# Attention with a coarse path, then a gated mixture of experts: v by one transfer for each head, coarse rows spread by one-hot products, constants from small bands

## The chip, the cores and the metric

One core of a Trainium2 chip runs the whole program. The metric is the device time of one execution in microseconds (us), lower is better. Fast runs of one kernel in one set of rounds agree within about 1.5%; between sets, on the same or another chip, the median of the kernel before moved. So kernels are compared by their ratio to the kernel before, run in the same rounds on the same chip.

The engines, as the page of the changed kernel shows them: PE runs 7566 products (PEld is its loading of weights, as many), DVE 470, ACT 403 and POOL 319 other instructions (sums, copies, casts, exponentials), SP only issues transfers here (DMA). Each engine works off its own list of instructions in order; in the changed kernel, for example, ACT stands still for 20.7 us before one copy of a constant, with later work behind it.

## The reference, cut to what matters

```python
# q, k, v: 8 batches x 8 heads x 576 rows x 64
q_d, k_d, v_d = means of four neighbouring rows            # 144 coarse rows
out_up    = repeat(softmax_attention(q_d, k_d, v_d), 4)    # each coarse row serves four queries
out_local = softmax_attention(q, k, v, mask=|i - j| < 4)
x = (out_up + out_local) as 4608 rows of 512
e = argmax(x @ w_gate)                                     # one of 8 experts for each row
out[row] = softmax weight * sigmoid(x @ w_output_gate)[e] * (relu(x @ w1[e]) @ w2[e])
```

A wrong argmax sends a row to another expert. The kernel therefore carries most operands as a high and a low half of 16 bits.

## The kernel before

A unit is two heads of one batch: 32 units, four for each batch. Queries are cut into ten windows, and each window needs at most 64 rows of k and v. A list scheduler in the Python code fixes the order of all tasks on all engines when the program is built. The parts that matter:

```python
def load_v(u):                       # 6 transfers for a unit, issued by SP
    for h in range(2):
        for w0, w1, n in ((0, 9, 2), (1, 2, 4), (5, 6, 4)):
            nc.sync.dma_start(vf[r, w0:...:w1 - w0, :], ...)

def upsample(b, t):                  # 10 transfers for a batch, also issued by SP:
    for w in (2 * t, 2 * t + 1):     # each normalised coarse row is copied to four queries
        nc.sync.dma_start(t_up[r:r + 4 * (j1 - j0), t, :], _ap(src, [src.ap[0], [0, 4], [1, Dm]]))

def x_sum(b, t):                     # mostly on POOL
    (nc.vector if t in XS_DVE else nc.gpsimd).tensor_tensor(x, x, t_up[:, t], op=ALU.add)

def make_mask():                     # 20 selects of POOL, then 22 more and 11 memsets for the means
    for w in range(NW):
        nc.gpsimd.affine_select(out=reg, ...); nc.gpsimd.affine_select(out=reg, ...)
# ... cut: casts and turns of q and k, means of v, scores, exponentials, values, gating, experts
```

The softmax here doesn't subtract the row's maximum and nothing guards it: scores larger than these inputs give would overflow.

## Time and profile before

| | kernel before |
|---|---|
| median of its runs | 543.5 us (539.1 to 546.8) |
| profiled execution | span 562.9 us, marked slow |
| first to last exponential | 32.66 to 338.86 us, 9.88 us a unit |
| last exponential to first product of the experts | 56.4 us |
| experts | 167.7 us |

There is one exponential pair for each unit, so the time between two of them is the pace of the attention. The profile's chain of work that ended last goes back from the last instruction and says at each step what released it. Its shares by engine (SPq is time in which a transfer was being issued, "issue" is time in which an engine waited for nothing that the profile shows):

```profile
PE 31%; DMA 17%; issue 17%; DVE 12%; POOL 10%; SPq 8%; ACT 2%; another core or an unknown queue 1%; POOLq 0%; DVEq 0%; ACTq 0%
```

A quarter of the whole span is transfers and their issue.

### The profile page before, as it was taken

To read this page: it belongs to the slowest core of one execution; us is meant where nothing else is said; L and a number is where in the kernel's file an instruction comes from. 1 tells how busy PE (TensorE), PEld (TensorE's weight loads), DVE (VectorE), ACT (ScalarE), POOL (GpSimd) and SP (SyncE) were. 2 spreads that over 40 slices of the span, in tenths; PEclk is the share of its full clock that TensorE was granted. 3 is DMA by queue.
4 is the path that set the end of the run, shared out by engine and by line. 5 is a ranking of instruction groups with operands and counts; after the bars stand their busy time and mean duration, and the time that the engine had idled before them with its cause. 6 is when DMAs were issued, how large, how long until landed. Compare 5 with 4: busy or idle time off the path is not lost.

```text
span 562.9 us, 17377 instructions
## 1 busy us (share of the span) xinstructions
PE 399.3 (71%) x7470; PEld 291.4 (52%) x7470; DVE 261.9 (47%) x480; ACT 227.4 (40%) x397; POOL 274.0 (49%) x351
## 2 busy tenths in 40 slices
PE   0457858548846869764778974530899999999992
PEld 0356746446634667653567753430655665565560
DVE  1457537329467665639655774431322332232220
ACT  0255444444624545633446562330233333333331
POOL 8863236319365655546746357484053345323312
PEclk9999795787865876975887786555799999999997
DMA  8569878988866984797853041513189999992202
GB/s 172 131 128 251 214 190 207 185 192 160 186 129 146 185 169 116 154 171 153 206 112 91 13 79 70 86 43 113 42 177 193 209 188 223 193 223 98 110 29 74
DMA packets 92743, 81.74 MB, mean 145 GB/s; under 512 B 49693, under 2 KB 80413, under 8 KB 92656
## 3 DMA queue, kind: packets, MB, share of 16 engines
q1 hardware_dynamic: 74736, 49.55, 38.6%
q0 software_dynamic: 17920, 30.98, 26.8%
q8 instruction: 60, 0.98, 0.7%
q14 instruction: 27, 0.22, 0.1%
HBM read 68.23 MB, written 21.05 MB: 159 GB/s over the span
## 4 chain that ended last, share of the span: by engine, by line
PE 31%; DMA 17%; issue 17%; DVE 12%; POOL 10%; SPq 8%; ACT 2%; another core or an unknown queue 1%; POOLq 0%; DVEq 0%; ACTq 0%
DMA vf<-in_v_dram 8%; PE pu L689 8%; PE py L699 6%; SPq L398 5%; DMA t_up<-xo 5%; POOL out_dram L702 3%; SPq L236 3%; PE ps L310 3%; PE t L261 2%; PE po L359 2%; PE pd L287 2%; PE ps L312 2%; DMA qk<-in_q_dram 2%; DVE xo L387 2%; POOL hx_xs L517 2%
## 5 line engine op out<-in xcount | busy, mean ns | idle before, releaser
L242 POOL CAST qk<-qk 96x768 f16<-96x768 f32 x64 | 59.1, 945 | 52.0 <-PE t L264 40.3
L402 POOL TENSOR_TENSOR xo<-xo,t_up 128x512 f32<-128x512 f32 x32 | 41.1, 1292 | 74.3 <-DMA t_up<-xo 74.1
L689 PE MATMUL pu<-xgT,w1sb 128*128 128x320 f16 x512 | 72.4, 303 | 1.7 <-DVE xgT L681 0.9
L699 PE MATMUL py<-w2sb,hs 128*128 128x512 f16 x320 | 70.4, 379 | 0.0
L702 POOL DMA_INDIRECT out_dram<-y,xg x40 | 39.7, 993 | 59.1 <-ACT y L701 57.3
L261 PE MATMUL t<-pm,qk 96*128 96x144 f16 x384 | 44.7, 268 | 27.6 <-POOL qk L242 19.4
L689 PEld LDWEIGHTS <-w1sb 128*128 128x128 f16 x512 | 50.7, 99 | 22.6 <-issue 2.7
L408 POOL TENSOR_TENSOR t_xl<-xo,xh 128x512 f16<-128x512 f32 x40 | 47.4, 1200 | 26.9 <-ACT xh L405 26.7
L692 ACT ACTIVATE hs<-pu 128x320 f16<-128x320 f32 x64 | 28.0, 438 | 68.3 <-PE pu L689 60.8
L328 ACT ACTIVATE eh<-ps 128x1008 f16<-128x1008 f32 x32 | 32.3, 1011 | 48.6 <-PE ps L310 41.5
L694 DVE TENSOR_SCALAR hs<-pu 128x320 f16<-128x320 f32 x64 | 31.5, 492 | 43.0 <-PE pu L689 36.6
L699 PEld LDWEIGHTS <-hs 128*128 128x128 f16 x320 | 31.3, 98 | 36.5
L681 DVE COPY xgT<-tp 128x1024 f16<-128x1024 f16 (+1 forms) x24 | 13.0, 595 | 74.7 <-PE py L699 60.1
L261 PEld LDWEIGHTS <-qk 96*128 96x128 f16 x384 | 31.4, 116 | 30.6 <-POOL qk L242 19.4
L701 ACT ACTIVATE y<-py,xg 128x512 f32<-128x512 f32 x40 | 27.5, 688 | 47.9 <-PE py L699 47.9
L517 POOL DMA_INDIRECT hx_xs<-xh,pos x40 | 40.0, 1001 | 12.1 <-issue 9.9
L287 PEld LDWEIGHTS <-pv 64*128 64x128 f16 x1280 | 27.8, 108 | 33.7 <-issue 31.2
L287 PE MATMUL pd<-t_vh,pv 64*128 64x64 f16 x640 | 31.1, 211 | 18.7 <-DVE vdl L299 8.1
L334 DVE TENSOR_TENSOR el<-ps,eh 128x1008 f16<-128x1008 f32 x32 | 38.4, 1200 | 7.9 <-ACT ps L329 6.6
L287 PE MATMUL pd<-vl,pv 64*128 64x64 f16 x640 | 30.9, 211 | 11.0 <-issue 7.4
L387 DVE TENSOR_TENSOR xo<-po,rs 128x448 f32<-128x448 f32 x64 | 36.9, 618 | 1.5
L203 POOL DMA_DIRECT2D w1sb<-in_moe_w_dram x16 | 11.9, 750 | 49.7 <-PE pu L689 49.7
(118 smaller groups left out, 870.3 us busy)
## 6 DMA issues: line engine op xcount, KB each, us to landing
qk<-in_q_dram SPq DMA_DIRECT2D x32, 288.0 KB
qk<-in_k_dram SPq DMA_DIRECT2D x32, 288.0 KB
vf<-in_v_dram SPq DMA_DIRECT2D x128, 64.0 KB
w1sb<-in_moe_w_dram POOLq DMA_DIRECT2D x16, 512.0 KB
w2sb<-in_moe_w_dram POOLq DMA_DIRECT2D x16, 512.0 KB
t_up<-xo SPq DMA_DIRECT2D x48, 120.0 KB
hx_xs<-zt SPq DMA_DIRECT2D x8, 645.0 KB
xg<-hx_xs SPq DMA_DIRECT2D x8, 645.0 KB
```

What stands on the lines that cost most here:

```text
L242: nc.gpsimd.tensor_copy(t16.rearrange("p m h d -> p h m d"), d["f", i])
L261: nc.tensor.matmul(tf[:, S // 2:S // 2 + SD], lhsT=t16[:, m, :], rhs=pm[:, m, :], start=(m == 0), stop=(m == 5), skip_group_check=True)
L287: nc.tensor.matmul(pd[:, h, c:c + D], lhsT=pv[r, w, :], rhs=m[r, w, 0:D], start=(w == 0 and i == 0), stop=(w >= NW - 2 and i == 1), skip_g ...
L328: nc.scalar.activation(d["eh"], ps, AF.Exp, scale=scale)
L334: nc.vector.tensor_tensor(d["el"], d["ps"][:, :, 0:NH], d["eh"], op=ALU.subtract)
L387: nc.vector.tensor_tensor(xo_s[b][:, :, c:c + D], po[:, h, :, 0:D], _bc(rs[:, h], D), op=ALU.mult)
L402: (nc.vector if t in XS_DVE else nc.gpsimd).tensor_tensor(x, x, t_up[:, t], op=ALU.add)
L408: nc.gpsimd.tensor_tensor(t_xl[:, t], xo_s[b][:, t, :], xh_s[b % 4][:, t, 0:Dm], op=ALU.subtract)
L517: ins = nc.gpsimd.indirect_dma_start(out=xs_dram.ap(), out_offset=bass.IndirectOffsetOnAxis(ap=gs[n]["pos"][:, c:c + 1], axis=0), in_=xh_s ...
L689: nc.tensor.matmul(pu[:, 0:c1 - c0], lhsT=w1sb[:, c, 128 * f:128 * f + 128], rhs=xgT[:, c, c0:c1], start=(c == 0), stop=(c == 3))
L699: nc.tensor.matmul(py, lhsT=hs[:, f, 128 * j:128 * j + 128], rhs=w2sb[:, f, :], start=(f == 0), stop=(f == NG - 1))
L702: ins = nc.gpsimd.indirect_dma_start(out=out_rows, out_offset=bass.IndirectOffsetOnAxis(ap=xgi[:, j, Dm // 2 + 1:Dm // 2 + 2], axis=0), in ...
```

## The change

The intent: fewer and simpler things on SP's queue, so that a load never stands behind the spreading of a finished batch. Ten windows of 57 queries (60 at the ends) put the rows of v at equal steps, so one transfer serves a head. The coarse rows reach their queries by products with one-hot matrices. The mask and the means come from one small band each. With it came a re-tuned order, shared tiles in PE's result memory (PSUM), both copies of the turned q and k on ACT, and part of the last batch's work moved from POOL to DVE.

```diff
-QN = [60, 56, 58, 58, 56, 56, 58, 58, 56, 60]
+QN = [60] + [57] * 8 + [60]
@@ load_v
-            for w0, w1, n in ((0, 9, 2), (1, 2, 4), (5, 6, 4)):
-                nc.sync.dma_start(vf[r, w0:w0 + (w1 - w0) * (n - 1) + 1:w1 - w0, :], ...)
+                nc.sync.dma_start(vf[r], _ap(s, [[D, 64], [57 * D, NW], [1, D]], -D))
@@ upsample
-            nc.sync.dma_start(t_up[r:r + 4 * (j1 - j0), t, :], _ap(src, [src.ap[0], [0, 4], [1, Dm]]))
+        ms = [(g, x) for g in range(2) if (t, g) in up_m for x in ("xdh", "xdl")]
+        for i, (g, x) in enumerate(ms):
+            nc.tensor.matmul(ps, lhsT=up_m[t, g], rhs=st[x, b][:, g, :], start=(i == 0), ...)
@@ x_sum
-        (nc.vector if t in XS_DVE else nc.gpsimd).tensor_tensor(x, x, t_up[:, t], op=ALU.add)
+        nc.vector.tensor_tensor(x, st.pop(("us", b, t)), x, op=ALU.add)
@@ constants: make_band, make_mask, make_means, spread_means in place of 42 selects with their memsets
+    def make_up():     # six one-hot matrices, five instructions each, on POOL
@@ order and tiles
-    XT_ACT = (1, 3, 4)
+    XT_ACT = (1, 3)
-    ROOM = {"T": 2, "S": 2, "O": 1, ...
+    ROOM = {"T": 2, "S": 3, "xd": 2, ...
... (cut: turn and turned in one tile, the scheduler's priorities, low halves of the last batch)
```

## The prediction

> **What bounds the kernel now.** I read first the page's busy shares and its 40 slices, then the stretches, the chain of work that ended last, and last the waits and the timeline of single engines.
>
> ```profile
> PE 399.3 (71%) x7470; PEld 291.4 (52%) x7470; DVE 261.9 (47%) x480; ACT 227.4 (40%) x397; POOL 274.0 (49%) x351
> PEclk9999795787865876975887786555799999999997
> DMA  8569878988866984797853041513189999992202
> ```
>
> No engine is full. The 40 slices (14.1 us each) show two stages: up to about 390 us attention and gating (32 units of two heads, eight batches of four units), then the experts, where PEclk is 9. The stretches view puts numbers on it (PE, PEld, DVE, ACT, POOL busy, clock, DMA share, GB/s):
>
> ```profile
> 30.00:340.00 310.00, 224.00 (x6133) 181.37 (x6133) 191.62 (x318) 156.17 (x266) 162.16 (x159) 0.78 0.73 155
> 395.00:563.00 168.00, 0.96 0.65 145
> ```
>
> In attention all four engines are busy 50 to 72% of the time, at a clock of 0.78. The change touches only this stage; the 168 us of experts stay. In the chain cut to 33 to 340 us, transfers and their issue lead:
>
> ```profile
> by line: DMA vf<-in_v_dram 15.6%; SPq L398 8.7%; DMA t_up<-xo 8.3%; issue 6.9%; SPq L236 4.7%; PE ps L310 4.7%; PE t L261 4.4%; PE pd L287 3.6%; PE ps L312 3.3%; DMA qk<-in_q_dram 3.2%; PE po L359 3.2%; DVE d L454 2.8%; PE t L264 2.7%; DVE
> ```
>
> vf, t_up, qk and the issues L398 and L236 make 40.5% of 307 us, 124 us. The queue that issues them (SP), its waits, and who waits for it:
>
> ```profile
> L236 SPq DMA_DIRECT2D vf<-in_v_dram x192: 595/614/1698, 3.9 to 304.2; - x192
> L398 SPq DMA_DIRECT2D t_up<-xo x80: 815/848/1505, 75.2 to 362.5; - x80
> SPq L398 <- DVE xo L387: 40.7, 3, 24.0
> POOL xo L402 <- DMA t_up<-xo: 74.1, 19, 11.4
> DVE xo L402 <- DMA t_up<-xo: 48.6, 8, 10.6
> ```
>
> An issue takes 0.61 or 0.85 us whatever its size, so at the medians SP needs 192 x 0.614 + 80 x 0.848 + 64 q/k x 0.43 + 8 fills x 0.69 = 219 us. It is in order: once a batch ten t_up issues wait for the normalised rows and hold back every load behind them. The exponentials show the result (start us, us):
>
> ```profile
> 233.14 1.01 ACT L328 ACTIVATE eh<-ps 128x1008 f16<-128x1008 f32 x1 [0.24 <-PE ps L310]
> 252.02 1.00 ACT L328 ACTIVATE eh<-ps 128x1008 f16<-128x1008 f32 x1
> ...
> 305.43 1.01 ACT L328 ACTIVATE eh<-ps 128x1008 f16<-128x1008 f32 x1 [0.64 <-PE ps L310]
> ```
>
> and, in the chain around the 19 us hole,
>
> ```profile
> 232.57 10.30 DMA vf<-in_v_dram
> ...
> 247.56 3.18 DMA t_up<-xo
> ...
> 251.64 7.18 DVE d L454
> ```
>
> Inside a batch units come every 5.0 to 6.9 us; the mean from the first exponential (32.66) to the last (338.86) is 306.2 / 31 = 9.88 us. So the round trip through SP bounds attention, not an engine.
>
> [...] The new transfer has the same 256-byte runs, so I expect issue time to fall and engine time for v not to. The trace agrees that issue is per transfer: transfers of 32 to 645 KB cost about 0.4 to 0.85 us each. [...]
>
> **The change part by part.**
> *v loads.* 192 issues become 65. 127 x 0.614 = 78 us leave SP. Packets stay 40,960 of 256 B. In 3 to 20 us (89.1% of 16 engines, 6,042 packets, nearly all q, k and v) a packet took 40 ns[...].
> *Spreading.* 80 issues x 0.848 = 68 us leave SP, with 9.4 MB. What remains on SP is 65 x 0.61 + 64 x 0.43 + 5.5 = 73 us, none waiting for results of the batch. Added a batch: 12 matmuls of 512 columns (six tile/half pairs, high and low part; 12 x 0.216 = 2.6 us at full clock), one 72x1024 ACT cast (about 1.0 us, like L328's 1008 elements), two 72x512 subtractions on POOL (about 1.2 us, as L408), and five sums on DVE (about 0.70 us, L402's least on DVE 0.691) in place of four on POOL (1.29) and one on DVE.
> *Turning q and k.* One PSUM tile per unit, both copies on ACT: 32 x (0.752 + 0.295) = 33.5 us leave DVE. ACT's rows give 576 elements 0.639, 1024 elements 1.014: 1152 take about 1.12, the small copy about 0.41, so 1.53 for 0.93, +0.60 a unit.
> *PSUM.* Two S, one O and T for turning become three shared S tiles; T serves spreading, turning x, logits and ranks.
> *Constants.* Masks and means in before run on POOL from 12.6 to 27.6 us, split by four casts; scores first end at 32.6. The new order has 13 selects and memsets for these but puts six one-hot matrices (30 small instructions, about 0.18 us each, 5.5 us) before the first cast. So casts begin at about 20 us, as before (18.6), but no longer break off: first exponential at about 26.5, 6 us gained.
>
> Work per unit afterwards, at these durations. PE at full clock: q/k 1.48, means 0.69, scores 1.20, values 1.40, plus a quarter of a batch's x turning 2.75, logits 1.6, ranks 0.3, spreading 2.6 (1.8): 6.6 us. DVE: 1.06 + 0.41 + 1.20 + 1.48, plus (5 x 0.70 + 3 x 0.685) / 4 and gating about 40 / 32: 6.8 (before 7.0). ACT: 0.74 + 1.53 + 0.38 + 2.02, plus (1.0 + 3.1 + 2.0 + 0.55) / 4: 6.3. POOL: 1.89, plus (6.0 + 2.4 + 6.5) / 4 and 0.2 of weights: 5.8. Four engines near 6.5 in static order never overlap perfectly; I choose 7.7 us a unit, 0.9 over the longest, because PE also shows gaps put down to issue (31.2 us before L287) that the change leaves. That is my main judgement.
>
> *The tail.* From the last normalisation (354.3) to the last logits copy (377.9) takes 23.5 us, of which 8 are t_up issue and landing and the rest sums alternating with low parts on POOL. Afterwards: cast 1.0, low 1.2, then five tiles in a pipeline with 7 us each on DVE and POOL: about 12.5. Gained 11.
>
> *Sum.* The profiled execution (562.9) is marked slow and is 19.4 us over the median of the timed runs. The experts run at 0.96 there, so I put that excess on attention: pace in timed runs about 9.88 - 19.4 / 31 = 9.25. Gain 31 x (9.25 - 7.7) = 48, plus 6, plus 11 = 65. 543.5 - 65 = 479 (rounded).
>
> **The rivals.** *A, DMA stays the bound.* For it: DMA share 0.73 with the same 256-byte packets, and chain pieces "DMA vf" of 10 us. Against: many of these pieces end at SP's next issue, not at an engine[...]. It would leave vf's 48 us on the chain: about 510 to 515. *B, DVE or PE with the shared PSUM becomes the bound.* Each unit now takes an S tile four times; held about 3.2 (q/k), 1.7 (means), 4.7 (scores), 3.1 (values), 12.7 / 3 = 4.2 us a unit unqueued, but with queueing this could double, and PE, in order, waits at each. Pace 8.6 to 9: 507 to 519. *C, better than I say.* [...] pace 7.0, 457. B and C are both likelier than A.
>
> **Range and chances.** Pace 7.0 to 8.6 gives 457 to 507; this is the range. Missing 2% (533) would take a pace above 9.4, and slower needs a new serial wait per batch as long as the old. Faster 0.96, same 0.03, slower 0.01.
>
> **What would show it.** Right: exponentials evenly spaced near 7.7 us with no hole over 12; SP issues of v about 0.6 to 0.7 us each, so longer transfers cost no more to issue; no wait for t_up; x sums on DVE near 0.7 us; first exponential near 26.5; clock in attention above 0.85; experts 168 us. Wrong: v issues growing with size, long waits of casts to f16 for vf (A), PE idle waiting for DVE or ACT to free S tiles with pace above 8.6 (B), or a cast start far after 20 us.

The sum came to 543.5 - (48 + 6 + 11) = 478.5, rounded up to 479.

- The 0.216 us of a product of 512 columns is measured: in the trace before, the 320 products L699 start 216 ns apart in the median.
- In that trace, between 3 and 20 us, the packets of 256 bytes took 22 ns on average (3959 of them) and those of 1.5 KB 97 (1536). By these I estimate (1280 x 22 + 384 x 97) / 16 = 4.1 us for a unit's loads, which is under every pace that the prediction weighs; so the argument against rival A holds.
- Rival C: its pace of 7.0, and with it the lower end of the range, is the author's guess.

## The result, and the profile after

The changed kernel took 503.7 us in the median of four runs (500.5 to 506.5), against 543.5 for the kernel before. The ratio of fast runs is 0.927, with a 95% interval of 0.918 to 0.936. A ratio here is the mean time of one kernel's fast runs over that of the other's fast runs of the same rounds, so it is not quite the ratio of the quoted medians. The prediction of "faster" was right, and 503.7 lies inside its range of 457 to 507, but near the upper end and 25 us above the 479.

| | before | after | predicted |
|---|---|---|---|
| first exponential | 32.66 | 34.62 | 26.5 |
| us a unit, first to last exponential | 9.88 (slow) | 8.35 | 7.7 |
| last exponential to first product of the experts | 56.4 | 43.7 | 45 |
| experts | 167.7 | 167.4 | 168 |

The page of the changed kernel: busy shares, granted clock and DMA share in 40 slices of 12.6 us, and the chain by engine.

```profile
PE 402.2 (80%) x7566; PEld 285.9 (57%) x7566; DVE 241.0 (48%) x470; ACT 245.1 (49%) x403; POOL 244.5 (48%) x319
PEclk9997595985979999597799995659999999999996
DMA  7599994796823899764970011141999999963211
PE 53%; issue 23%; POOL 11%; DVE 7%; ACT 2%; DMA 1%; POOLq 0%; SPq 0%; DVEq 0%; ACTq 0%
```

DMA and SPq fell from a quarter of the chain to 1%. PE and "issue" now hold three quarters of it. The clock still drops to 5 in several slices of the attention. The stretches view of attention and of experts (PE, PEld, DVE, ACT, POOL busy, clock, DMA share, GB/s):

```profile
30.00:320.00 290.00, 245.17 (x6474) 189.43 (x6471) 184.86 (x328) 183.57 (x283) 161.41 (x160) 0.82 0.67 146
337.00:504.00 167.00, 152.28 (x992) 92.17 (x992) 44.54 (x88) 55.50 (x104) 55.16 (x60) 0.96 0.65 146
```

PE is busy 85% of the attention, but at a clock of 0.82. Next, the view of v's tile (minimum, median and maximum of one issue in ns) with SP's two largest waits in the attention, from its waits view (total us, times, longest), and the group of the sums with spread rows (busy us, mean ns, idle before).

```profile
L267 SPq DMA_DIRECT2D vf<-in_v_dram x63: 595/636/3122, 3.1 to 255.6; - x63
SPq L253 <- POOL qk L272: 87.8, 33, 8.8
SPq L267 <- DVE vl L282: 63.9, 18, 13.1
L437 DVE TENSOR_TENSOR xo<-us,xo 128x512 f32<-128x512 f32 x40 | 26.7, 685 | 13.9 <-PE us L433 13.9
```

One issue of v still costs 0.64 us although it carries 160 KB. SP now waits because no buffer is free, which means that loads run ahead of the work. In the kernel before, SP's largest wait was for the normalised rows (40.7 us), and it waited for free buffers of q and k for 29.2.

**Where 8 us went at the start.** POOL's timeline (start us, duration us), then ACT's longest wait before 35 us, then the first exponential on ACT's timeline:

```profile
14.04 0.51 POOL L100 MEMSET mk<- 64x504 f16 x1
14.49 0.20 POOL L143 MEMSET up<- 72x128 f16 x1
...
22.25 0.51 POOL L100 MEMSET mk<- 64x504 f16 x1
22.82 3.74 POOL L272 CAST qk<-qk 96x768 f16<-96x768 f32 x4
```

```profile
ACT mk L103 <- POOL mk L100: 20.7, 1, 20.7
34.62 1.03 ACT L357 ACTIVATE eh<-ps 128x1008 f16<-128x1008 f32 x1
```

The six one-hot matrices occupy POOL from 14.5 to 22.2 us, between the two halves of the mask. The casts of q and k stand behind them, and so does ACT, which takes its instructions in order and waits for the second half of the mask.

**Where the pace went.** Two places on PE's timeline, before and after a stop:

```profile
40.26 0.21 PE L295 MATMUL tqk<-id,qk 96*128 96x96 f16 x1
44.13 0.58 PE L295 MATMUL tqk<-id,qk 96*128 96x96 f16 x5 [3.67 <-issue]
...
108.25 0.19 PE L394 MATMUL po<-t_vd,el 128*128 128x65 f16 x1
111.74 0.24 PE L394 MATMUL po<-t_vd,eh 128*128 128x65 f16 x1 [3.30 <-issue]
```

In the first, PE has done one of six transposes of one tile and stops for 3.7 us. The other five need nothing that the first did not have. In the second it stops inside the twelve products of one unit's values. No other engine ended these stops. The waits view of PE between 35 and 294 us says the same of most of the rest (its waits put down to issue add up to 31.9 us, those for DVE to 7.0):

```profile
PE pd L316 <- issue: 10.8, 7, 2.4
PE tqk L295 <- issue: 6.6, 3, 3.7
PE tqk L292 <- issue: 4.2, 3, 2.7
PE tqk L292 <- DVE xo L416: 3.9, 5, 1.0
```

And the stretches around the same two stops (the third number from the right is the clock):

```profile
36.00:40.40 4.40, 3.83 (x133) 3.02 (x130) 2.22 (x4) 4.34 (x6) 1.65 (x2) 1.00 1.23 201
40.50:44.10 3.60, 0.00 (x0) 0.00 (x0) 2.62 (x3) 0.00 (x0) 0.82 (x1) 0.66 1.26 190
44.20:48.40 4.20, 4.20 (x107) 2.91 (x109) 0.00 (x0) 3.10 (x4) 0.82 (x1) 0.50 1.09 257
111.80:127.00 15.20, 15.20 (x216) 10.12 (x217) 8.98 (x14) 7.14 (x11) 7.54 (x8) 0.50 0.78 145
```

The clock is 1.00 before the stop and 0.50 after it. After the second stop it stays at 0.50 for 15 us, in which PE is busy all the time; the turning products L292 then start 120 ns apart (from 115.4 us), against 62 at a clock of 1.00 (from 39.2 us). The clock halved 1.2 us after the first of these stops had begun, and also in a stop of 2.6 us (from 49.4 us) and 0.6 us after one of 1.5 us (from 240.9 us). Eight such periods of half clock in the attention add up to about 85 us.

What stands beside the stops is a queue of its own that the page lists as "instruction", with 61 packets of 16,384 bytes. I worked the following out of the trace's records. PE ran 2 x 7566 = 15,132 products and weight loads, 248 for each of these packets; in the kernel before it was 249 (14,940 and 60 packets), in e7, below, 244 (10,268 and 42). Taking stops of PE and PEld together that last over 0.7 us and lie between 30 and 300 us, there are 18 of them. Fifteen end 1.2 to 1.7 us after the end of such a packet. They stand in many different tiles, but at one place in the count of the program: if PE's recorded instructions (15,164 with its waits and branches) are numbered from 0 in order of start, 14 of the 18 stops end with an instruction whose number leaves the remainder 193 when divided by 256. So these 14 lie multiples of 256 instructions apart. From all this I infer that the packets are the fetches of PE's program, that one brings a block of 256 instructions, and that PE stops where a block ends; what a packet holds, the trace doesn't say. A second profile of the same kernel has 15 such stops; 12 of them end 1.3 to 1.6 us after a packet, and these are the 12 that stand at block ends. The kernel before had such stops too (10 of them, 22.0 us in all up to its last normalisation).

**Theory (T1),** to be tested below: the attention is now bound by PE. PE takes short instructions faster than they are fetched while data transfers fill the DMA engines (share 0.71 between 35 and 294 us). It stops for want of instructions, and the clock is lower where it stops (1.00 before the stop at 40.5 us, 0.50 after it). **Rival T2** (rival B of the prediction): the shared PSUM tiles and the waits of engines for each other bound the pace. **Rival T3** (close to rival A): units still wait for data to land. The changed kernel's own waits already speak against both rivals: between 35 and 294 us, PE waited 7.0 us for DVE, and the waits of all engines for landed data add up to 5.3 us, none of them of a cast of v.

### The profile page after: what moved, and what is told of

The parts are those of the page before. It is cut to its first block, busy times and chain, and to the rows that moved or that the text cites. A ratio compares the mean times of both kernels' runs of the same rounds, so it can differ in the third digit from the quotient of the medians.

```text
span 504.7 us, 17116 instructions
## 1 busy us (share of the span) xinstructions
PE 402.2 (80%) x7566; PEld 285.9 (57%) x7566; DVE 241.0 (48%) x470; ACT 245.1 (49%) x403; POOL 244.5 (48%) x319
## 4 chain that ended last, share of the span: by engine, by line
PE 53%; issue 23%; POOL 11%; DVE 7%; ACT 2%; DMA 1%; POOLq 0%; SPq 0%; DVEq 0%; ACTq 0%
PE pu L730 9%; PE py L740 7%; PE tqk L292 5%; PE ps L339 4%; PE po L388 4%; PE us L433 4%; PE pd L316 4%; POOL out_dram L743 4%; PE tqk L295 3%; PE po L394 3%; PE ps L341 3%; POOL hx_xs L552 3%; PE po L404 2%; PE tp L448 2%; DVE xo L416 2%
## 5 line engine op out<-in xcount | busy, mean ns | idle before, releaser
L272 POOL CAST qk<-qk 96x768 f16<-96x768 f32 x64 | 57.2, 904 | 95.7 <-issue 48.6
L730 PEld LDWEIGHTS <-w1sb 128*128 128x128 f16 x512 | 50.5, 99 | 22.2 <-issue 2.7
L316 PE MATMUL pd<-t_vh,pv 64*128 64x64 f16 x640 | 28.3, 201 | 36.9 <-ACT t_vh L277 25.1
L735 DVE TENSOR_SCALAR hs<-pu 128x320 f16<-128x320 f32 x64 | 31.5, 492 | 42.4 <-PE pu L730 36.0
L303 ACT COPY qkT<-tqk 128x1152 f16<-128x1152 f16 x32 | 35.8, 1119 | 30.3 <-PE tqk L295 30.3
L552 POOL DMA_INDIRECT hx_xs<-xh,pos x40 | 41.8, 1044 | 17.2 <-issue 8.3
L316 PEld LDWEIGHTS <-pv 64*128 64x128 f16 x1280 | 24.8, 102 | 41.8 <-issue 23.3
L443 POOL TENSOR_TENSOR t_xl<-xo,xh 128x512 f16<-128x512 f32 x38 | 44.1, 1184 | 8.0 <-ACT xh L440 7.8
L292 PE MATMUL tqk<-pm,qk 96*128 96x144 f16 x384 | 40.2, 249 | 8.3 <-issue 4.2
L282 DVE SCALAR_TENSOR_TENSOR vl<-vf,t_vh 128x640 f16<-128x640 f32 x32 | 36.7, 1159 | 11.0 <-ACT t_vh L277 11.0
L413 DVE RECIPROCAL rs<-po 128x14 f32<-128x14 f32 x32 | 7.8, 245 | 63.1 <-PE po L404 63.1
L357 ACT ACTIVATE eh<-ps 128x1008 f16<-128x1008 f32 x32 | 32.5, 1016 | 9.5 <-PE ps L339 8.8
L295 PE MATMUL tqk<-id,qk 96*128 96x96 f16 x384 | 31.6, 225 | 6.6 <-issue 6.6
```

What stands on the lines that cost most here:

```text
L272: nc.gpsimd.tensor_copy(t16.rearrange("p m h d -> p h m d"), d["f", i])
L282: nc.vector.scalar_tensor_tensor(d["vl"], in0=d["vf"], scalar=VS, in1=d["vh"][:, :, 0:D], op0=ALU.mult, op1=ALU.subtract)
L292: nc.tensor.matmul(tf[:, i, S // 2:S // 2 + SD], lhsT=t16[:, m, :], rhs=pm[:, m, :], start=(m == 0), stop=(m == 5), skip_group_check=True)
L295: nc.tensor.transpose(tf[:, i, :].bitcast(F16)[:, 96 * m:96 * m + 96], t16[:, m, :], id16[0:96, 0:96])
L316: nc.tensor.matmul(pd[:, h, c:c + D], lhsT=pv[r, w, :], rhs=m[r, w, 0:D], start=(w == 0 and i == 0), stop=(w >= NW - 2 and i == 1), skip_g ...
L443: (nc.vector if b == B - 1 and t % 2 else nc.gpsimd).tensor_tensor(t_xl[:, t], xo_s[b][:, t, :], xh_s[b % 4][:, t, 0:Dm], op=ALU.subtract)
```

## The experiments

All twelve runs, below the first measurement; "in" gives the kernel before in the same rounds. Runs with one execution have no interval and an unknown state, and only their traces are used. The gaps are PE's stops over 0.7 us from 30 us on, worked out as above and followed to some 25 us after the last exponential: their sum, the part that has an instruction packet beside it (under way in the stop or in the half us before it), and the part that stands at a block end (remainder 193, one more or less allowed). In the changed kernel a packet comes every 5.5 us, so being beside one says little by itself; the third number says more.

| run | us (in) | ratio, 95% interval | first exp. | us a unit | gaps, beside packets, at block ends |
|---|---|---|---|---|---|
| after, first measurement | 503.7 (543.5) | 0.927, 0.918 to 0.936 | 34.6 | 8.35 | 38.4, 37.6, 31.5 |
| e1_start | 498.1 (547.1) | 0.913, 0.907 to 0.919 | 30.9 | 8.23 | 33.6, 30.3, 27.0 |
| e2_spans | 499.5 (547.1) | 0.915, 0.909 to 0.921 | 34.6 | 8.20 | 32.9, 28.5, 25.9 |
| e3_spread | 568.0 (547.1) | 1.038, 1.031 to 1.046 | 32.5 | 10.16 | 95.6, 58.1, 26.1 |
| e4_quiet | one run | | 34.1 | 6.94 | 18.4, 18.4, 5.9 |
| e5_start2 | 494.9 (544.2) | 0.907, 0.901 to 0.913 | 27.7 | 8.37 | 32.7, 32.7, 24.4 |
| e6_ten | 526.3 (544.2) | 0.965, 0.959 to 0.971 | 32.7 | 9.10 | 74.7, 53.1, 38.5 |
| e7_half_pe | one run | | 32.5 | 7.11 | 24.6, 12.4, 5.6 |
| e8_traffic | one run | | 35.7 | 9.43, then 7.10 | 33.3, 31.6, 25.5 |
| e9_after | 502.6 (548.6) | 0.917, 0.911 to 0.922 | 34.6 | 8.38 | 34.6, 34.6, 28.8 |
| e10_late | 498.3 (548.6) | 0.905, 0.899 to 0.912 | 34.7 | 8.04 | 37.8, 29.7, 24.9 |
| e11_both | 499.6 (548.6) | 0.903, 0.897 to 0.909 | 27.7 | 8.38 | 35.0, 27.8, 22.6 |
| e12_three | 494.8 (548.6) | 0.902, 0.897 to 0.907 | 28.7 | 8.27 | 31.1, 24.1, 19.6 |

The changed kernel itself came out at 0.927 in one set of rounds and 0.917 in another (e9_after, its own repetition). So a difference of one per cent between runs of different sets is not a result. e1 to e4 shared one set on one chip; e5 to e8 and e9 to e12 were two sets on another chip.

### What undoing each part costs

**e2_spans: v by three transfers again.**

```diff
-                nc.sync.dma_start(vf[r], _ap(s, [[D, 64], [57 * D, NW], [1, D]], -D))
+                for w0, n in ((0, 2), (2, 4), (6, 4)):
+                    nc.sync.dma_start(vf[r, w0:w0 + n, :], _ap(s, [[D, 64], [57 * D, n], [1, D]], (57 * w0 - 1) * D))
```

> v is again loaded with three transfers for each head, of 2, 4 and 4 spans; all else is the changed kernel. Theory T1 (the attention is now bound by PE and its supply of instructions, and the queue of SP runs ahead): 503 to 508 us, pace 8.3 to 8.5 us. Rival (the smaller number of issues was itself the gain): 515 us or more, and SP's issues stand on the chain of waits again.

There is no loss: the ratio is 0.915, as good as the changed kernel's in either set, and 499.5 us lies below the 503 to 508 that T1 expected. The view of v's tile shows three times the issues at the same price:

```profile
L268 SPq DMA_DIRECT2D vf<-in_v_dram x189: 595/611/1693, 3.1 to 259.2; - x189
```

SP spends 189 x 0.611 = 115 us on them instead of 63 x 0.636 = 40, and the time does not get longer: SP had waits to spare. So the rival falls: with the spreading off SP, fewer issues of v are worth nothing. What they would be worth beside the old spreading was not run.

**e3_spread and e6_ten: spreading by transfers again.** e3 puts back the transfers and POOL's sums. The new windows do not begin at multiples of four, so a batch takes 22 transfers.

```diff
-            nc.tensor.matmul(ps, lhsT=up_m[t, g], rhs=st[x, b][:, g, :], ...)
+            nc.sync.dma_start(t_up[r0:r0 + n, t, :], ...)            # first rows of a broken group
+            nc.sync.dma_start(t_up[r:r + 4 * m, t, :], ...)          # whole groups of four
+            nc.sync.dma_start(t_up[r + 4 * m:r + 4 * m + n, t, :], ...)  # last rows
-        nc.vector.tensor_tensor(x, st.pop(("us", b, t)), x, op=ALU.add)
+        (nc.vector if t == 2 else nc.gpsimd).tensor_tensor(x, x, t_up[:, t], op=ALU.add)
```

> The means' rows are spread over the queries by transfers again (22 for a batch instead of 10, since the new windows don't begin at multiples of four), summed on POOL except for one group of five; all else is the changed kernel. If the round trip of these transfers was what bounded the kernel before: once for each batch a hole of over 12 us between exponentials, pace 9 us or more, total 522 to 540. Rival (the single transfers of v brought the gain, and the spread could have stayed): 510 us or less.

It took 568.0 us, 4% longer than even the kernel before, and above the expected 522 to 540. e6 tells whether the 22 transfers or the round trip did it: it leaves out the broken groups.

```diff
-            nc.sync.dma_start(t_up[r0:r0 + n, t, :], ...)
-            nc.sync.dma_start(t_up[r + 4 * m:r + 4 * m + n, t, :], ...)
```

> Wrong in a few rows on purpose: as e3_spread, but only the whole groups of four queries are spread, so that a batch has 10 transfers as in the kernel before and not 22. e3 took 568.0 us against 547.07. If the dearer part of e3 was the round trip (once per batch): 545 to 560 us, holes for each batch as in e3. If it was the number of issues on the queue of SP: 520 to 535 us.

526.3 us, a ratio of 0.965 (the result is wrong in the rows left out, as meant). That is the band expected if the number of issues was the dearer part. So e3's surplus over e6 was the number of transfers. The comparison that counts is e6 against the changed kernel: 0.965 against 0.917 to 0.927, or some 21 to 26 us of 545. That is what the one-hot products, with their sums on DVE, saved against ten transfers a batch with four of five sums on POOL. The largest waits of the kind in e6, of POOL and of SP between 33 and 315 us:

```profile
POOL xo L435 <- DMA t_up<-xo: 34.5, 15, 8.0
SPq L431 <- DVE og L525: 25.8, 1, 25.8
SPq L431 <- DVE xo L418: 18.8, 3, 16.2
```

POOL's wait for t_up and SP's for the normalised rows (xo L418) were in the prediction's account of the kernel before, and both are gone in the changed one. The profile puts SP's longest wait down to an instruction of the gating (og), which the spreading does not read; that one was not explained. The remaining 18 us between the kernel before and e6 (544.2 and 526.3) belong to the rest of the change (v by one transfer, order, tiles, constants, the last batch's split), which I did not take apart further.

### What bounds the pace now

**e4_quiet: the same work without loads.** From the third unit on, every unit computes with the q, k and v of the first two.

```diff
+        if u >= 2:
+            st.setdefault(u, {})["f", i] = fix[u % 2, i]
+            return
```

> Wrong result on purpose: all units from the third on compute with the q, k and v of the first two, and no other q, k or v is loaded; every instruction of PE, DVE, ACT and POOL stays. The experts get the same rows eight times over, so only the attention is read. T1 (instruction fetches of PE are delayed by data transfers, leave gaps[...]): PE's gaps over 0.7 us shrink from 38 us to under 12, the clock of the stretch rises from 0.82 to over 0.93, pace about 7 us. T2 (shared PSUM tiles and waits between engines in order bound it): pace stays within 0.3 of 8.35 us, with gaps that other engines end.

The pace is 6.94 us, as T1 said, with every instruction of PE, DVE, ACT and POOL still there. T2 needed 8.35 and falls. The gaps shrank to 18.4 us, not below 12 as expected. But only 5.9 us of them stand at block ends, where the changed kernel had 31.5; what ends the other 12.5 us was not looked into. The stretches from first to last unit, the changed kernel's in the first fence and e4's in the second:

```profile
35.00:294.00 259.00, 219.82 (x5931) 170.62 (x5928) 164.23 (x285) 169.06 (x257) 139.94 (x140) 0.84 0.71 154
```

```profile
34.00:249.00 215.00, 196.24 (x5919) 155.76 (x5920) 170.49 (x283) 168.53 (x257) 138.23 (x141) 0.94 0.24 45
```

Divided by 31 units, PE is busy 7.09 us in the one and 6.33 in the other, at clocks of 0.84 and 0.94, and idle 1.26 and 0.61. So of the 1.4 us between the two paces about half is a slower clock and half is standing still.

**e8_traffic: the loads made, but nobody waits for them.** They go into tiles that nothing reads.

```diff
+        if u >= 2:
+            st.setdefault(u, {})["f", i] = fix[u % 2, i]
+            f = sbA.tile([96, 2, 6, D], F32, tag=f"un{i}", name=f"un{i}", bufs=2)   # the transfer goes here
```

> Wrong result on purpose: as e4_quiet, every unit from the third on computes with the q, k and v of the first two, but all loads are still made, into tiles that nothing reads, so no engine waits for them and they run as fast as the queues let them, in the first half of the attention. If traffic by itself slows PE's supply: in the stretch with loads the pace is 8 us or more with gaps beside fetches, in the later stretch without them about 6.9 us as in e4 (6.94). If e4 was fast because nobody waited for a landing: 6.9 us all along.

This run holds both cases in one execution. The loads had landed by about 170 us. Its stretches from the first exponential to the fifteenth, and from there to the last:

```profile
35.72:167.70 131.98, 105.06 (x2507) 79.86 (x2505) 67.15 (x113) 74.34 (x110) 50.76 (x51) 0.75 1.13 228
167.70:288.36 120.66, 112.98 (x3419) 90.12 (x3418) 97.29 (x172) 95.12 (x149) 89.72 (x90) 0.94 0.32 64
```

With traffic 14 units took 131.98 us, 9.43 each. Without it 17 units took 120.66 us, 7.10 each. The order of the units does not explain this: in e4 the same two stretches went at 6.65 and 7.18 us a unit. No engine waited for the landing of these loads, so T3 falls as the cause of this difference: it is the traffic itself, here denser (DMA share 1.13) than in the changed kernel (0.71). PE's gaps are 23.7 us in the first stretch (1.7 a unit) and 6.2 in the second (0.4 a unit), of which 23.0 and 2.5 stand at block ends, and the clock is 0.75 and 0.94.

The records show the instruction packets, too. Each time PE passes a block end, the next packet follows. It starts 3.19 us later in the first stretch (median of 20) and 0.95 us later in the second (median of 26), and takes 1.26 and 1.06 us on average. So under traffic the packet is late mostly because it starts late; behind what it waits was not looked into. The median packet ends 4.7 us after the block end with traffic and 2.0 without, and the stops above end some 1.4 us after the packet. PE runs (5931 + 5928) / 31 / 256 = 1.5 blocks a unit, so by e4's 6.33 us a block lasts it 4.2 us: I estimate 6.1 us for a new block with traffic, longer than PE needs for one, and 3.4 without, shorter.

**e7_half_pe: fewer instructions of PE.** The low halves are left out of the values and the means of v.

```diff
-            return [(o, a_h, m_h, start), (o[:, 0:D], a_h, m_l, False), (o, a_l, m_h, False)]
+            return [(o, a_h, m_h, start)]
-            for i, m in enumerate((d["vh"], d["vl"])):
+            for i, m in enumerate((d["vh"],)):
```

> Wrong result on purpose (low halves left out): PE does a third of the products of the values and half of those of the means of v, about 100 matmuls a unit instead of some 176; DVE, ACT, POOL and the transfers do what they did. T1 (PE and its instruction supply bound the attention): fewer fetches, PE's gaps beside fetches fall from 38 us to under 15, pace falls to 6 to 7.3 us, where ACT or DVE or the transfers take over. T2 (PSUM tiles and in-order waits): pace stays over 8 us.

There were 42 instruction packets instead of 61, the gaps beside them fell from 37.6 to 12.4 us (those at block ends from 31.5 to 5.6), and the pace to 7.11 us, as T1 expected. This run alone doesn't part the two halves of T1, because PE also has less to do, and faster units packed the transfers closer (DMA share 0.88, clock 0.80 over 32.5 to 253 us). The result still passed the comparison with the reference on this draw, in 463 us by one run. I don't count it as a better kernel, since it gives up the precision that the high and low halves were built for, and one draw doesn't show that it can be spared.

### The start

**e1_start: the one-hot matrices later.**

```diff
-    task(("upm", 0), "POOL", 4.0, 2, [], make_up)
+    for i in range(len(UPS)):
+        task(("upm", i), "POOL", 1.3, -1 + 0.5 * i, [("cast", 1, 2 + i)], make_up, i)
```

> The six one-hot matrices are built one at a time, each after a later cast, instead of in one block of about 7.7 us ahead of the second mask memset on POOL. Theory (the late start is that block): the first exponential comes at about 27 us instead of 34.62, the pace and the tail stay, total about 496 against 503.7. Rival (something else sets the start, the first q and k transfers for instance): the first exponential stays later than 32 us and the total within 2 us of 503.7.

The casts began at 15.2 instead of 22.8 us, but the first exponential came at 30.87 and not at 27. PE's first task in its order was the means of v. They waited for ACT, and ACT for memsets that DVE did late. So neither the 27 of the theory nor the rival's "later than 32" came true, and the ratio of 0.913 (0.907 to 0.919) is not to be told apart from the changed kernel's 0.917.

**e5_start2: those chains taken apart too.**

```diff
-            (nc.vector if g else nc.gpsimd).memset(mk[r, g, :], 32.0)
+            nc.gpsimd.memset(mk[r, g, :], 32.0)
-        nc.vector.memset(pv[r], 0.0)
+        (nc.gpsimd if h else nc.vector).memset(pv[r], 0.0)
@@ means of v after the first turn; ACT's halves of the constants after the first turned copy
```

> e1 moved the casts from 22.8 to 15.2 us, but the first exponential only to 30.87: PE's first task in its order was the means of v, which waited for ACT, and ACT for memsets on DVE. Here besides e1 the memsets of the second half of both constants move to POOL, PE turns q and k of unit 0 ahead of the means of v, and ACT fills its halves of the constants after the first turn. If the start is these in-order chains: first exponential at 24 to 27 us, about 5 us less than e1 in total (ratio to the kernel before about 0.904 against e1's 0.913). Rival (the transfers themselves are late): no change from 30.87.

The first exponential is at 27.65 us, just past the expected 24 to 27:

```profile
27.65 1.01 ACT L359 ACTIVATE eh<-ps 128x1008 f16<-128x1008 f32 x1 [1.07 <-PE ps L341]
```

Whether the time followed is unclear: the ratio is 0.907 (0.901 to 0.913) against e1's 0.913, with overlapping intervals, from different sets. In the two profiled executions it did not: the ninth exponential comes at 94.4 us in e5 and at 94.8 in e1, so the 3.2 us had been given back within eight units, in which the queues are full (DMA share 0.92 and 0.97 from 30 to 100 us). From the first exponential to 95 us, POOL's waits for landed q and k add up to 5.5 us in e5 and 1.7 in e1, while the stops at block ends are no longer (8.5 and 9.2). That points to the landing of loads, but it was not tested.

### Towards a better kernel

**e9_after** repeats the changed kernel as the measure for the last three.

> The changed kernel itself again, so that e2 and the combinations are read against it on one chip. Expected as in its first measurement: a ratio to the kernel before of 0.92 to 0.935.

It gave 0.917 (0.911 to 0.922), slightly below the expected band.

**e10_late: the weights of the first experts later.**

```diff
-            u = 7 + 6 * e + i
+            u = (21, 26, 28)[e] + i
```

> The changed kernel, only the weights of the first three experts (12.6 MB) are asked for later: after units 21 to 24, 26 to 29 and 28 to 31 instead of 7 to 10, 13 to 16 and 19 to 22, so that most of them falls in the last units and the tail, where the transfer queues stood idle. If traffic slows PE's supply (e8: 9.43 us a unit with loads, 7.1 without), 5 to 12 us less than the changed kernel of the same rounds, most of it between 100 and 260 us. Rival (only waits for landings matter): no change, or a loss when the experts begin.

The ratio went from 0.917 to 0.905, about 6 us, with intervals that just touch. The clock between 100 and 260 us rose from 0.82 to 0.93, where the traffic was taken away, and the last exponential came at 284.0 instead of 294.4. Part of it was lost afterwards: 44.9 instead of 43.2 us to the experts, and more in them.

**e11_both** has e5's start and e10's weights, **e12_three** also e2's three transfers.

> The start of e5 and the later weights of e10 together, right in every row. If both gains stand by themselves: 12 to 20 us less than the changed kernel of the same rounds (ratio to the kernel before 0.89 to 0.905). If the earlier start is given back in the stretch with dense traffic, as e5's pace of 8.37 against e1's 8.23 hints: only e10's gain and 3 to 6 us.

> As e11, with v by three transfers for each head as in e2, which took 499.5 us where the changed kernel would have had some 507 on that chip. If single transfers of v are worth nothing: within 4 us of e11. If one long transfer is worse [...]: 3 to 8 us less than e11. If the saved issues count once the rest is faster: 5 us or more longer.

e11 came out at 0.903 and e12 at 0.902: the earlier start adds nothing that these runs can show, and three transfers of v are again no worse than one. e12 is the fastest right kernel here, 494.8 us where the changed kernel took 502.6 and the kernel before 548.6. Its interval lies below the changed kernel's. By the ratios it is 1 - 0.902 / 0.917 = 1.6% faster.

## Why the prediction was right or wrong

- **SP's round trip bounds the kernel before: right in kind, and shown for about half of the gain.** Putting the spreading back on the queue cost 21 to 26 us (e6, ten transfers) of the 40 us gained, or 61 to 66 (e3, 22 transfers), and with it came back the waits for t_up. The rest of the gain was not taken apart.
- **192 issues of v become 65 and 78 us leave SP: right in count, wrong in worth.** The issue price held (0.64 us). But e2 shows that none of these 78 us was on the path once the spreading had left the queue. The prediction did not say how the gain splits between the two parts.
- **Single durations: right; sums of work per unit: too high for three engines.** Sums on DVE took 0.685 us (predicted 0.70), turned copies on ACT 1.12 and 0.41 us (the same), the experts 167.4 us (168). But busy times from the first exponential to the experts (34.62 to 337.29 us), divided by 32 units, are 5.8 us for DVE (predicted 6.8), 5.6 for ACT (6.3) and 5.1 for POOL (5.8). PE, put at 6.6 at full clock, was busy 7.5 us at a clock of 0.80. So PE alone was the longest, and not DVE.
- **One reading of the prediction to put right; it changes no conclusion.** Rival A's 48 us on the chain would give 479 + 48 = 527, not 510 to 515.
- **Pace 7.7 from "0.9 over the longest": the step that was mis-sized.** It measured 8.35, so 31 x 0.65 = 20 us of the 25 missed. PE's sum was sound: without traffic the same instructions ran at 6.94 us a unit, with PE busy 6.33 of it at a clock of 0.94. What failed was the allowance of 0.9 us. It named gaps put down to issue, but took them for a fixed remainder. Most of them stand where PE's fetched blocks end (31.5 us in the changed kernel, 5.9 without loads in e4), where the next packet starts late under data traffic (3.19 us after the block end in e8, 0.95 without), and with them came a lower clock (0.84 against 0.94). The pace lies just under rival B's 8.6 to 9, but B's mechanism fell with e4.
- **"Clock in attention above 0.85" and "no hole over 12": wrong.** The clock was 0.82 (30 to 320 us), and five holes of 12.3 to 14.5 us remained.
- **First exponential at 26.5: wrong by 8 us.** The term was the six one-hot matrices at 5.5 us "before the first cast". They took 7.7 us, and what they stood before was also the second half of the mask, behind which ACT waited in order. Moving the matrices (e1) brought the first exponential to 30.9, and taking the other in-order chains apart as well (e5) to 27.7, so both together are shown to be the cause. How much of those 8 us reaches the end is unclear: e5's ratio is 0.010 under e9's, some 5 us, with overlapping intervals, and e11's only 0.002 under e10's.
- **Tail 45 us: right in sum, only partly in reason.** It measured 43.7. From the last normalisation to the experts it went from 40.9 us (a slow execution) to 32.5 us, and in e6, with transfers, it was 37.4. So the one-hot products account for about 5 of these 8, by one profiled execution each. Another 4 us came ahead of that point, between last exponential and last normalisation (15.4 to 11.2), which the prediction did not see.
- **The sum:** 8 late at the start, 20 from the pace, less 2 in the tail, turn 479 into 505; measured 503.7. The prediction put the slow profile's excess on the attention, and this balance gives no reason against that.

**What stays open.** That fetches end most of the stops is inferred. It rests on their place (14 of 18 multiples of 256 instructions apart), on the fixed lag of 1.2 to 1.7 us after a packet, and on e8, where the packets start later with traffic than without (3.19 and 0.95 us after a block end). Why they start later is not shown, and I could not slow or speed the fetch alone. The stops at other places are not explained. That the stops bring the clock down is only seen in order of time: each of the eight periods at half clock begins inside a stop or at most 0.7 us after one, but other stops were followed by none.

## What to carry to other kernels

When a serial round trip through a transfer queue is taken away, ask next how fast PE can be fed: here some 190 products a unit, most of them short, used up a block of the program in some 4.2 us, and a new one took some 6.1 under traffic (my estimates from e4 and e8, above). Look then for PE stops inside one tile that the profile puts down to issue, number PE's instructions, and see whether the stops lie at even distances, as 14 of 18 did here, at multiples of 256. A part of a change that frees an engine which afterwards only waits can be worth nothing, as the 78 us of e2 were, and putting that part back alone is the quickest way to see it.
